# In float32 groups GpSimd multiplies the exponentials by the reciprocals of their sums, in place of VectorE

## The chip, the cores and the metric

The kernel runs on one core of one Trainium2 chip. The metric is the time of the device in microseconds: the median of several executions of the whole program. A core has a matrix engine (TensorE, in rows PE, and PEld for its weight loads), VectorE (DVE), ScalarE (ACT), GpSimd (POOL) and a queue engine that issues most transfers (SyncE, SP). Each engine takes its instructions in the order of the program, and waits for other engines by semaphores.

## The reference

Three stages follow each other, all in float32. The inputs are `q`, `k` and `v` for 4 sequences of 576 tokens with 8 heads of 64 (2304 tokens in all), and six weight matrices.

```
scores = scale * q @ k^T, masked to the last 64 positions of each row
attn   = exp(scores - max);  attn = attn / (sum(attn) + 1e-9)
x      = (attn @ v) as 2304 x 512
x      = ((x @ w1) * (x @ w2)) @ w3 @ w_out
h      = x @ w_in;   out = (h * sigmoid(h)) @ w_out2
```

The change concerns the division by the sum.

## The kernel before

**Groups.** Attention is cut into 72 groups: 18 blocks of 128 tokens by 4 pairs of heads. The first 17 groups (`plain(g)`, `PLAIN = 17`) multiply in plain float32 on TensorE; the others split each operand into a high and a low part. The change concerns the first 17 alone, "float32 groups". A group goes through these steps, each a function:

- `scores(g)`: TensorE's product (L313) into PSUM; VectorE adds the mask, scales, and takes the row's extreme, in two instructions (L327), one per head.
- `exps(g)`: ScalarE takes the exponentials in place in the tile `sm`, 128 x 2 x 192, and their sums (L338).
- `normalise(g)`: VectorE adds 1e-9 to the sums (L346), takes the reciprocals `rs` (L348), and multiplies the 384 columns of `sm` by them, each head's by its own reciprocal (L350). The second operand is `rs`, repeated 192 times along the row.
- `transposes(g)`: TensorE turns `sm` in three parts (L360), and in `split_t(g)` ScalarE copies the result out (L366).
- `values(g)`: TensorE's product with `v` (L387 to L389), copied to `xr` by ScalarE (L390).

**Their order.** The order of the program is written out by hand. `half(2g)` issues `scores(g)`, `values(g-2)`, `transposes(g-1)` with its copy, and `exps(g)`; `half(2g+1)` issues `normalise(g)` and loads for later groups. So on TensorE the transposes of a group stand behind the scores of the next group, and on ScalarE the exponentials of group g stand behind the copy of group g-1.

**The work around them.** In the first stretch, `phase_w` (some 95 us), the weights arrive as 64-bit floats and are converted to float32, 512 columns at a time: two scalings on ScalarE (L119, L120), a shift and a merging of the sign on VectorE (L130, L133), and an integer add on GpSimd (L137). Some chunks then get a high and a low part (L145 on ScalarE; L149 on VectorE or GpSimd in turn). TensorE meanwhile multiplies `w3` by `w_out` (L542). The halves of the groups 0 to 13 are spread over this stretch; the groups 14 to 16 fall into the next one, `phase_a(0)`, where TensorE's products with `w1` and `w2` begin (L576). GpSimd also takes the low parts of `x` there and here (`split`, L84).

**What fills the gaps.** A chunk's second stage is not issued at once. It is put into a list, `parts`, as two pieces: `fraction` (L130) and `sign`, and `fill()` issues the next piece. `sign` issues the merging on VectorE and, right behind it, the add on GpSimd:

```
nc.vector.scalar_tensor_tensor(out=b, in0=self.high, scalar=-0x80000000, in1=self.z, ...)
nc.gpsimd.tensor_tensor(out=x, in0=b, in1=self.r, op=ALU.add)
```

`normalise` calls `fill()` ahead of each of its three instructions.

Of the kernel before, what the change touches and what calls it, by code (L numbers as in the profile page):

```python
# [14 lines left out]
ALU = mybir.AluOpType  # L15
# [27 lines left out]
def tile_window_attention_ffn(ctx, tc, qkv, vp, mask, ident, w1, w2, w3t, w_out, w_in, w_out2, out):  # L43
# [7 lines left out]
    nc = tc.nc  # L51
# [153 lines left out]
    def fill(n=1):  # L205

        for _ in range(min(n, len(parts))):
            parts.pop(0)()
# [44 lines left out]
    def plain(g):  # L253


        return g < PLAIN
# [85 lines left out]
    def normalise(g):  # L342
        _, rs = s_st.pop(g)
        x = sm[g % 2]
        fill()
        nc.vector.tensor_reduce(out=rs, in_=sums_of[g % 2], axis=mybir.AxisListType.X, op=ALU.add)  # L346
        fill()
        nc.vector.reciprocal(out=rs, in_=rs)  # L348
        fill()
        nc.vector.tensor_tensor(out=x, in0=x, in1=rs.unsqueeze(2).to_broadcast([128, 2, 192]), op=ALU.mult)  # L350

    def transposes(g):

# [56 lines left out]
    def half(h):  # L410
# [18 lines left out]
        else:  # L429
            if g < NG:  # L430
                normalise(g)
# [639 lines left out]
```

## Time and profile before

| what | value |
|---|---|
| median of 3 runs | 844.87 us (844.01 to 845.13) |
| the profiled execution's own time | 844.38 us |
| its span in the profile | 842.6 us |
| TensorE busy | 824.5 us (98%) |
| VectorE busy | 614.4 us (73%) |
| ScalarE busy | 560.8 us (67%) |
| GpSimd busy | 530.6 us (63%) |

The span runs from the first to the last instruction of the program. A busy time is the union of an engine's instructions; TensorE's matmuls are pipelined and their ends are modelled, so that a high share says that it is rarely without work and not that it is at its peak. The shares are means over stages that differ: the changed line runs in the first 112 us alone.

### The profile page before, as it was taken

Reading aid. Unit: us, or ns where it says so; the run is one execution under the profiler, and the core shown is the slowest. Engines: PE = TensorE matmul, PEld = TensorE weight load, DVE = VectorE, ACT = ScalarE, POOL = GpSimd, SP = SyncE. Lnnn points to the kernel's source line nnn. Section 1 sums busy time; section 2 is a strip of 40 time slices with the busy share of each in tenths; the row PEclk is TensorE's granted clock in tenths of the full one; section 3 lists DMA queues with packets and bytes.
Section 4 is the critical chain, followed back from the end, with each engine's and each line's share of the span. In section 5 each row is a group of like instructions: output and inputs, shape, how many; then the busy total and the mean of one; then the engine's idle time right before and its main releaser. Section 6 shows DMA issues by size and latency. Waiting matters only on the chain.

```text
span 842.6 us, 14171 instructions
## 1 busy us (share of the span) xinstructions
PE 824.5 (98%) x4410; PEld 744.9 (88%) x4410; DVE 614.4 (73%) x1420; ACT 560.8 (67%) x1389; POOL 530.6 (63%) x588
## 2 busy tenths in 40 slices
PE   5999999999999999999999999999999999999998
PEld 2555799999999999999999998888898888888986
DVE  5879877688888888888368698998644568644544
ACT  5889778898898899898556566546543446443433
POOL 5669676677677677677465577876455457454441
PEclk9999999999999999999999999999999999999999
DMA  8999334434544554543443522301301201201001
GB/s 299 315 309 289 106 96 125 145 118 142 167 157 144 170 157 145 169 152 107 134 154 114 200 75 75 125 26 51 101 25 45 106 26 63 88 25 51 1 1 75
DMA packets 57130, 102.66 MB, mean 122 GB/s; under 512 B 5472, under 2 KB 34912, under 8 KB 57056
## 3 DMA queue, kind: packets, MB, share of 16 engines
q1 hardware_dynamic: 53600, 97.05, 35.7%
q10 hardware_dynamic: 3456, 4.72, 1.5%
q8 instruction: 35, 0.57, 0.3%
q14 instruction: 39, 0.32, 0.1%
HBM read 88.11 MB, written 13.63 MB: 121 GB/s over the span
## 4 chain that ended last, share of the span: by engine, by line
PE 68%; ACT 7%; POOL 6%; issue 4%; DVE 3%; ACTq 0%; POOLq 0%; DVEq 0%
PE o L835 22%; PE ab L576 16%; PE hy L781 11%; PE hx L781 9%; PE x L600 6%; POOL klo L296 2%; ACT sm L338 1%; PE t L360 1%; POOL xr L406 1%; POOL vhl L84 1%; ACT qkhi L292 1%; PE o L394 1%; POOL p L84 1%; PE s L317 1%; POOL q L84 1%
## 5 line engine op out<-in xcount | busy, mean ns | idle before, releaser
L835 PE MATMUL o<-hl,gp 128*128 128x512 f32 x504 | 133.3, 394 | 0.0
L576 PE MATMUL ab<-xa,hl 128*128 128x384 f32 x576 | 119.0, 341 | 0.0
L781 PE MATMUL hy<-xop,j 128*128 128x384 f32 x576 | 116.0, 335 | 0.5 <-DVE tmp L675 0.5
L576 PE MATMUL ab<-xb,hl 128*128 128x384 f32 x576 | 115.4, 334 | 0.0
L84 POOL TENSOR_TENSOR gp<-tmp,gp 128x384 fp32r<-128x384 f32 x56 | 63.5, 1134 | 79.5 <-ACT gp L81 77.9
L781 PEld LDWEIGHTS hy<-xop,j 128*128 128x128 f32 x576 | 102.7, 188 | 9.8 <-DVE tmp L675 1.6
L835 PEld LDWEIGHTS o<-hl,gp 128*128 128x128 f32 x504 | 93.1, 188 | 13.1
L576 PEld LDWEIGHTS ab<-xb,hl 128*128 128x128 f32 x576 | 101.3, 188 | 0.0
L797 ACT ACTIVATE tmp<-hx 128x384 f32<-128x384 f32 x48 | 23.6, 492 | 114.0 <-DVE hx L675 69.2
L576 PEld LDWEIGHTS ab<-xa,hl 128*128 128x128 f32 x576 | 99.1, 188 | 0.0
L675 DVE TENSOR_TENSOR tmp<-hy,tmp 128x384 f32<-128x384 f32 x96 | 53.2, 554 | 56.9 <-PE hy L781 52.0
L781 PE MATMUL hx<-xop,j 128*128 128x384 f32 x432 | 86.6, 335 | 0.0
L835 PE MATMUL o<-hl,gq 128*128 128x512 f32 x324 | 85.9, 393 | 0.0
L84 POOL TENSOR_TENSOR gq<-tmp,gq 128x384 fp32r<-128x384 f32 x36 | 40.0, 1111 | 72.6 <-ACT gq L81 72.6
L781 PEld LDWEIGHTS hx<-xop,j 128*128 128x128 f32 x432 | 76.8, 188 | 4.2
L406 POOL TENSOR_TENSOR xr<-ot 128x128 f32<-128x128 f32 x55 | 32.3, 587 | 73.9 <-DVE ot L405 65.8
L296 POOL TENSOR_TENSOR klo<-qk,qkhi 64x192 fp32r<-64x192 f32 x110 | 68.0, 618 | 7.6 <-ACT qkhi L292 2.7
L835 PEld LDWEIGHTS o<-hl,gq 128*128 128x128 f32 x324 | 60.3, 188 | 11.2
L600 PE MATMUL x<-p,wp 128*128 128x384 f32 x360 | 69.6, 339 | 0.0
L338 ACT ACTIVATE sm<-sm,nm 128x192 f32<-128x192 f32 x144 | 64.5, 450 | 3.8 <-DVE nm L327 2.4
L600 PEld LDWEIGHTS x<-p,wp 128*128 128x128 f32 x360 | 61.8, 188 | 0.0
L137 POOL TENSOR_TENSOR cv_b<-cv_b,cv_r 128x512 int32<-128x512 int32 x32 | 48.6, 1520 | 18.7 <-DVE cv_b L133 9.4
(138 smaller groups left out, 1887.4 us busy)
## 6 DMA issues: line engine op xcount, KB each, us to landing
qk<-in_qkv SPq DMA_DIRECT2D x55, 384.0 KB, 3.2
words<-in_w_out SPq DMA_DIRECT2D x24, 512.0 KB, 5.4
r<-w_in SPq DMA_DIRECT2D x22, 512.0 KB, 3.4
words<-in_w3t SPq DMA_DIRECT2D x16, 512.0 KB, 6.6
words<-in_w SPq DMA_DIRECT2D x16, 512.0 KB, 6.6
xe<-in_w_in SPq DMA_DIRECT2D x16, 512.0 KB, 4.6
v<-in_qkv SPq DMA_DIRECT2D x55, 96.0 KB, 2.7
x2d<-x2s ACTq DMA_DIRECT2D x24, 192.0 KB, 1.9
```

Of the source, the lines that this page charges most:

```text
L84: (nc.vector if eng_lo == "dve" else nc.gpsimd).tensor_tensor(out=lo, in0=src, in1=f32(hi), op=ALU.subtract)
L137: nc.gpsimd.tensor_tensor(out=x, in0=b, in1=self.r, op=ALU.add)
L292: nc.scalar.copy(out=hi, in_=t)
L296: nc.gpsimd.tensor_tensor(out=k_lo[g % 2][hs, h * 192 : h * 192 + 192], in0=t[hs, n], in1=f32(hi[hs, n]), op=ALU.subtract)
L338: nc.scalar.activation(out=x, in_=x, func=AF.Exp, scale=-1.0, bias=nm[:, h : h + 1], accum_out=sums_of[g % 2][:, h, 0:1])
L406: nc.gpsimd.tensor_tensor(out=xr[:, c, r : r + 128], in0=t[:, 0:128], in1=t[:, 128:256], op=ALU.add)
L576: nc.tensor.matmul(acc, lhsT=w[:, l, fs], rhs=x[k // 2][:, k % 2, r, :], start=(k == 0 and n == 0), stop=(k == 3 and n == 2),)
L600: nc.tensor.matmul(acc, lhsT=wp[f][:, l, o * 128 : (o + 1) * 128], rhs=p[f][:, r, :], start=(f == 0 and n == 0), stop=(f == 7 and n == 2),)
L675: eng.tensor_tensor(out=out, in0=a, in1=b, op=op)
L781: nc.tensor.matmul(bank[name], lhsT=w[:, l, at + kt], rhs=x[:, kt, r, :], start=(fresh and kt == 0 and n == 0), stop=(kt == 1 and n == 2), ...
L797: nc.scalar.activation(out=sg, in_=src, func=AF.Sigmoid)
L835: nc.tensor.matmul(oacc[t], lhsT=g[:, l, cols], rhs=weights["out", 2 * p + i][:, r, :], start=(p == 0 and i == 0 and n == 0), stop=(p == P ...
```

## The change

In the float32 groups the third instruction of `normalise` goes to GpSimd's queue. Operands, result and place in the program's order are the same; the other groups keep it on VectorE.

```diff
@@ -347,7 +347,9 @@
         fill()
         nc.vector.reciprocal(out=rs, in_=rs)
         fill()
-        nc.vector.tensor_tensor(out=x, in0=x, in1=rs.unsqueeze(2).to_broadcast([128, 2, 192]), op=ALU.mult)
+        (nc.gpsimd if plain(g) else nc.vector).tensor_tensor(
+            out=x, in0=x, in1=rs.unsqueeze(2).to_broadcast([128, 2, 192]), op=ALU.mult
+        )
```

## Rows read from the trace of the kernel before

**Rows 1.** The page: engine's busy time and share; TensorE's granted clock in 40 slices.
```profile
PE 824.5 (98%) x4410; PEld 744.9 (88%) x4410; DVE 614.4 (73%) x1420; ACT 560.8 (67%) x1389; POOL 530.6 (63%) x588
...
PEclk9999999999999999999999999999999999999999
```
**Rows 2.** Busy time by stretch: window, length, each engine's busy us (instructions), clock, DMA share.
```profile
60.00:70.00 10.00, 9.22 (x37) 5.20 (x36) 9.06 (x29) 9.73 (x27) 9.93 (x8) 1.00 0.92 294
70.00:80.00 10.00, 9.82 (x36) 5.32 (x34) 9.19 (x19) 8.75 (x21) 9.78 (x9) 1.00 0.89 287
...
120.00:140.00 20.00, 20.00 (x129) 20.00 (x128) 14.91 (x54) 16.23 (x49) 11.49 (x18) 1.00 0.35 103
```
**Rows 3.** Groups of the first 100 us: busy us, mean ns | idle before, releasers.
```profile
L137 POOL TENSOR_TENSOR cv_b<-cv_b,cv_r 128x512 int32<-128x512 int32 x14 | 20.1, 1435 | 10.0 <-DVE rs L348 3.6 <-DVE rs L346 2.7 <-ACT cv_r L120 2.3
...
L350 DVE TENSOR_TENSOR sm<-sm,rs 128x384 f32<-128x384 f32 x15 | 10.2, 677 | 0.5
...
L360 PE MATMUL t<-id_sb,sm 128*128 128x128 f32 x42 | 7.1, 278 | 3.8 <-DVE sm L350 1.5 <-ACT cv_b L119 1.3 <-ACT cv_r L120 0.8
...
L84 POOL TENSOR_TENSOR xa<-xr,xa 128x384 fp32r<-128x384 f32 x2 | 2.0, 1008 | 0.0
```
**Rows 4.** Order of time around group 1: start us, duration us, engine and line.
```profile
19.50 0.69 DVE L133 SCALAR_TENSOR_TENSOR cv_b<-words,cv_z 128x512 int32<-128x512 int32 x1
...
20.30 0.56 DVE L350 TENSOR_TENSOR sm<-sm,rs 128x384 f32<-128x384 f32 x1
20.34 1.66 POOL L137 TENSOR_TENSOR wo<-cv_b,cv_r 128x512 int32<-128x512 int32 x1 [0.35 <-DVE rs L348]
...
21.01 0.52 PE L360 MATMUL t<-id_sb,sm 128*128 128x128 f32 x3 [0.75 <-DVE sm L350]
...
23.35 0.42 ACT L366 COPY pw<-t 128x320 f32<-128x320 f32 x1
```
**Rows 5.** Order of time, VectorE: the multiplications of groups 5, 7, 8, 11, 13.
```profile
44.00 0.56 DVE L350 TENSOR_TENSOR sm<-sm,rs 128x384 f32<-128x384 f32 x1
...
55.17 0.56 DVE L350 TENSOR_TENSOR sm<-sm,rs 128x384 f32<-128x384 f32 x1
...
62.12 0.56 DVE L350 TENSOR_TENSOR sm<-sm,rs 128x384 f32<-128x384 f32 x1
...
79.03 1.35 DVE L350 TENSOR_TENSOR sm<-sm,rs 128x384 f32<-128x384 f32 x1
...
90.44 0.56 DVE L350 TENSOR_TENSOR sm<-sm,rs 128x384 f32<-128x384 f32 x1
```
**Rows 6.** Order of time, TensorE: transposes of groups 4, 5, 7, 8, 11, 13.
```profile
39.98 0.50 PE L360 MATMUL t<-id_sb,sm 128*128 128x128 f32 x3
...
45.02 0.50 PE L360 MATMUL t<-id_sb,sm 128*128 128x128 f32 x3
...
56.79 0.50 PE L360 MATMUL t<-id_sb,sm 128*128 128x128 f32 x3
...
62.82 0.52 PE L360 MATMUL t<-id_sb,sm 128*128 128x128 f32 x3 [0.78 <-ACT cv_r L120]
...
80.53 0.52 PE L360 MATMUL t<-id_sb,sm 128*128 128x128 f32 x3 [0.71 <-DVE sm L350]
...
94.35 0.50 PE L360 MATMUL t<-id_sb,sm 128*128 128x128 f32 x3
```
**Rows 7.** Order of time, GpSimd: two adds ahead of group 11's transposes.
```profile
78.70 1.26 POOL L137 TENSOR_TENSOR cv_b<-cv_b,cv_r 128x512 int32<-128x512 int32 x1
79.92 1.61 POOL L137 TENSOR_TENSOR q<-cv_b,cv_r 128x512 int32<-128x512 int32 x1
```
**Rows 8.** Order of time, ScalarE: copies of groups 4 and 7, exponentials of group 8.
```profile
40.52 0.43 ACT L366 COPY pw<-t 128x320 f32<-128x320 f32 x1
...
58.25 0.46 ACT L366 COPY pw<-t 128x320 f32<-128x320 f32 x1
60.20 0.46 ACT L338 ACTIVATE sm<-sm,nm 128x192 f32<-128x192 f32 x1 [1.49 <-DVE nm L327]
```

## The prediction

> **What bounds the kernel now.** I read the page first. TensorE is busy for 98% of the span and is granted nine tenths or more of its clock in every slice, the 2.4 GHz level [rows 1], so the time is TensorE's work plus its pauses: 842.6 - 824.5 leaves 18 us of pauses in all. An engine other than TensorE matters only where TensorE waits for it. Next I read the busy time by stretch: the changed line runs only in the first 112 us, where weight conversion, TensorE's float32 products and the 17 float32 groups run together. There TensorE still has small gaps, GpSimd varies between much room and none (9.93 and 9.78 busy of 10 between 60 and 80 us), and VectorE is above 8 of 10 [rows 2]. From 120 us on TensorE has no gap at all in the stretch shown [rows 2]. A pause added to TensorE before 112 us can therefore not be made good later: it is added to the end. The question is how long TensorE waits in front of the 17 sets of transposes.
>
> Third, the groups of instructions of the first 100 us [rows 3]. The transposes (L360) have 3.8 us of idle in front of them, mostly put down to the multiplication (L350). That is the price of the chain today. Fourth, the order of time around single groups, which carries the sum.
>
> **The pattern of one group.** In `normalise`, `fill()` stands between the reduction, the reciprocal and the multiplication. In the groups 1 to 13 one of these fills issues a `sign` part: its VectorE half (L133) runs between reduction and reciprocal, and its GpSimd half (the integer add, L137) is issued right behind it, thus ahead of the multiplication. Group 1 shows it [rows 4]: L133 19.50 to 20.19, reciprocal, L350 20.30 to 20.86, transposes at 21.01. GpSimd's add starts at 20.34, at the same moment as L350. On VectorE the multiplication doesn't see this add. On GpSimd it stands behind it.
>
> **The change, part by part.**
> Removed: 17 multiplications on VectorE. The unhindered one takes 0.56 us [rows 4]; the mean over the first 15 is 677 ns [rows 3]. Together 11.5 us of VectorE's time, none of it on TensorE directly.
> Added: 17 multiplications on GpSimd. The trace has no product on GpSimd, and none with an operand repeated along the row. The nearest row is the subtraction of the same 128x384 elements (L84), 1008 ns [rows 3]. I take 1.0 us. Below, the 0.56 us of VectorE bounds it; above I take 1.6 us, about the longest add of [rows 4], since nothing shows what the repeated operand costs. The Trainium skill speaks against the change: GPSIMD Engine Reference, 4.1 Engine selection, gives elementwise work on a tile to VectorE, with GpSimd about twice as slow for two inputs; 1.0 against 0.56 agrees, and with exactly twice the sum below would be some 1 us higher (an estimate).
> Moved: the wait. GpSimd now waits for the reciprocal; behind that wait stand only later adds, whose VectorE halves come later anyway. TensorE waits for GpSimd in place of VectorE. No DMA is moved.
> Given back: add and multiplication no longer stretch each other. In group 1 the add took 1.66 us because L350 ran [rows 4]; unhindered it is about 1.28 (the add at 78.70 took 1.26 [rows 7]). So GpSimd pays 1.0 and gets 0.38 back where they met. The Trainium skill (SBUF, State Buffer, section SBUF: two separate sides) says that VectorE with two SBUF inputs and GpSimd exclude each other for the whole instruction; the stretched add agrees. This gift is in the sum.
>
> **The payment of a group.** Count from the end of L133. Before: L350 ends 0.67 later (20.86 - 20.19), the transposes start 0.15 after that: 0.82. After: 0.15 from VectorE to GpSimd (20.19 to 20.34), the add 1.27, the multiplication 1.0, and 0.15 to TensorE: 2.57. The transposes become possible 1.75 us later. How much TensorE feels is 1.75 less the room that the group had: start of the transposes less the end of L350 less 0.15.
> The rooms, from the starts of L350 and of the transposes [rows 5, 6]: group 1 none; 5: 45.02 - 44.56 - 0.15 = 0.3; 7: 0.9; 8 none; 11 none; 13: 3.2. Worked out in the same way from the two views, groups 2, 3 and 12 have none, 4 has 1.25, 6 1.55, 9 0.85, 10 1.55; 0, 14 and 15 more than 1; 16 none, but its queue neighbour is short of the usual add, at most 0.6.
>
> **Who pays again.** If each group paid anew, the sum of 1.75 less room is 4 x 1.75 (groups 1, 2, 3, 8) + 2 x 1.75 (11, 12) + 0.5 + 1.45 + 0.2 + 0.85 + 0.9 + 0.2 + 0.6 = 15.2 us. That is the upper end. But once TensorE is late, a later group whose own chain isn't late hides the next delay. The link back is ScalarE's copy L366, which follows the transposes and stands ahead of the next group's exponentials.
> - Group 1 pays 1.75.
> - Groups 2 to 4 pay nothing: ScalarE reaches the copy at 23.35 [rows 4], 1.8 us after the transposes of group 1 were done (21.53), so the chain of group 2 keeps its time; TensorE, late by 1.75, meets a multiplication late by 1.75. Group 3 is the same; 4 has 1.25 of room and VectorE is behind there anyway.
> - From group 5 the copy follows at once (40.52 [rows 8], after transposes that end at 40.48 [rows 6]), chain and TensorE are late together: 5 pays 1.45, 6 0.2, 7 0.85.
> - Group 8: its exponentials wait at 60.20 for VectorE and not for the copy at 58.25 [rows 8], so the chain is less late than TensorE; against that GpSimd's queue is full. Walking the three queues forward, each row starting when its engine and its last input are ready, I get 1.0 of the 1.75. Groups 9 and 10 then pay 0.15 each by the same walk.
> - Group 11: two adds follow each other on GpSimd, at 78.70 and 79.92 [rows 7], the second ahead of the multiplication: 79.92 + 1.27 + 1.0 + 0.15 = 82.35 against 80.53: 1.8, and 0.4 for the queue that is full since 60 us [rows 2]. Group 12 follows from a chain less late than TensorE and pays nothing.
> - 13 to 16 pay nothing (room, or the same reason).
> Sum: 1.75 + 1.45 + 0.2 + 0.85 + 1.0 + 0.3 + 2.2 = 7.75 us. VectorE's freed time is inside it, as the slack of groups 4, 8 and 12.
> The profiled execution took 844.38 us (span 842.6 and 1.8 around it), the median is 844.87. 844.38 + 7.75 = 852.1, and 0.5 for the median: 852.6 us.
> Low bound of this case: groups 8 to 12 pay once 1.75 between them and the rest stands, 6.0 us: 850.9; with a multiplication of 0.8 us, 0.2 less at some nine paying places: 849.1. High bound: 1.3 us at the same places, 2.7 more: 855.3.
>
> **The rivals.**
> - *Every group pays anew* (15.2 us, 860.1): it needs every chain to be as late as TensorE. Against it stand the two ScalarE rows of groups 2 and 8. 0.06.
> - *The product with a repeated operand is dear on GpSimd*: at 1.6 us nine places pay 0.6 more, 7.75 + 5.4 = 13.2: 858.1. For it: no row shows this form. Against it: the subtraction over 384 and the add over 512 elements (1.0 and 1.27 us) differ as their widths do, whatever the operation. 0.10.
> - *Hidden anyway*, within 0.2% (1.7 us, about what a measurement of this kernel can tell from no change): the late transposes would have to fall into pauses that TensorE has for other reasons. Only the two waits not put down to L350, 1.3 and 0.8 [rows 3], offer that: 7.75 - 2.1 is still 5.6. 0.05; its time is 845.5.
> - *Faster*, the other side: VectorE, above 8 of 10 busy, is the real brake; its 11.5 us and GpSimd's 0.38 per meeting bring the adds earlier and the 3.8 us in front of L360 go: 841.0. It decides only if the multiplication ends less than 0.67 us after L133, which the add ahead of it (1.27) excludes in the groups 1 to 13. 0.05.
>
> **How the numbers follow.** The forecast case has 0.74. Slower: 0.74 + 0.06 + 0.10 = 0.90; same 0.05; faster 0.05. The range runs from 848.5, under the low bound, to 858.0, taking in most of the dear product; outside lie faster, same and the case in which each pays anew, 0.16, and some of the dear one.
>
> **What would show it.** The product on GpSimd at 1.0 us, starting where the add L137 ends and not at the reciprocal. The transposes waiting for GpSimd, with some 11.5 us of idle in front of them in place of 3.8. The copies and exponentials of groups 2 and 3 at their old times. GpSimd's adds at 1.28 in place of 1.66. From 120 us on everything shifted by one constant. The forecast is wrong if the product stands ahead of the add in GpSimd's queue (then it pays about 0.5 per group), or if it is not near 1.0 us.

## The result, and the profile after

| kernel | median (range), runs | ratio to before, 95% interval |
|---|---|---|
| before | 845.08 us (844.01 to 846.4), 6 | |
| changed | 853.07 us (850.92 to 854.2), 6 | 1.0096 [1.0085, 1.0107] |

The change costs 8.0 us. The profiled execution took 851.4 us, with a span of 849.6 where before had 842.6, 7.0 more. Executions of the changed kernel differ more among themselves than those of before, and in step with TensorE's mean clock: the one with a clock of 1.000 took 850.92, those with 0.995 to 0.997 took 852.85 to 854.2.

The page of the changed kernel, engines and granted clock, beside [rows 1]:

```profile
PE 826.7 (97%) x4410; PEld 745.8 (88%) x4410; DVE 603.2 (71%) x1403; ACT 561.5 (66%) x1389; POOL 538.8 (63%) x605
...
PEclk9999999999999999999999999999999999999999
```

VectorE lost 11.2 us of work, and GpSimd has only 8.2 us more, although 17 products (14.5 us) came to it: its adds no longer meet VectorE's multiplication, and the 40 adds L137 of the first 125 us take 51.5 us in place of 56.5. TensorE runs the same 4410 matmuls, but is busy 2.2 us longer. Of the 7.0 us of the span 4.8 are thus pauses, and the rest slower matmuls (shown below). The groups of the first 108 us (lines below the diff are two higher: L362 are the transposes, L368 the copy, L544 the products with `w_out`), beside [rows 3]:

```profile
L137 POOL TENSOR_TENSOR cv_b<-cv_b,cv_r 128x512 int32<-128x512 int32 x14 | 18.1, 1294 | 9.0 <-DVE rs L348 5.1 <-DVE rs L346 3.8 <-DVE cv_b L133 0.2
...
L350 POOL TENSOR_TENSOR sm<-sm,rs 128x384 f32<-128x384 f32 x15 | 12.8, 855 | 2.5 <-DVE rs L348 2.5
...
L362 PE MATMUL t<-id_sb,sm 128*128 128x128 f32 x45 | 7.9, 283 | 8.2 <-POOL sm L350 8.1
```

The pauses before the transposes went from 3.8 to 8.2 us, now put down to GpSimd's product. A product takes 0.82 us unhindered (855 ns in the mean), and the add of this row is at 1.29 in the mean where it was at 1.44. Group 1 in order of time, GpSimd and TensorE, beside [rows 4]:

```profile
21.02 1.27 POOL L137 TENSOR_TENSOR wo<-cv_b,cv_r 128x512 int32<-128x512 int32 x1 [0.47 <-DVE rs L348]
22.25 0.83 POOL L350 TENSOR_TENSOR sm<-sm,rs 128x384 f32<-128x384 f32 x1
...
23.13 0.55 PE L362 MATMUL t<-id_sb,sm 128*128 128x128 f32 x3 [2.25 <-POOL sm L350]
...
23.52 5.30 PE L544 MATMUL accw<-wo,q 128*128 128x512 f32 x8
```

The product starts as the add ends, at 22.25; the reciprocal was ready at 20.95. TensorE stands for 2.25 us, 1.50 more than before. The last row holds something that the prediction doesn't know: eight matmuls took 5.30 us, which took 3.60 before:

```profile
21.36 3.60 PE L542 MATMUL accw<-wo,q 128*128 128x512 f32 x8
```

Busy time by stretch, around it and in tens of us, the clock being the column after POOL's:

```profile
20.00:22.00 2.00, 0.88 (x7) 0.64 (x5) 1.61 (x5) 1.23 (x2) 1.52 (x2) 1.00 0.99 293
22.00:24.00 2.00, 0.87 (x5) 0.64 (x6) 1.85 (x6) 1.68 (x4) 2.00 (x3) 1.00 0.98 311
24.00:26.00 2.00, 2.00 (x4) 0.81 (x3) 0.92 (x4) 2.00 (x7) 0.31 (x2) 0.58 0.88 287
26.00:28.00 2.00, 2.00 (x4) 0.86 (x3) 1.40 (x3) 1.71 (x4) 2.00 (x2) 0.56 1.03 400
28.00:30.00 2.00, 2.00 (x11) 1.28 (x10) 1.72 (x5) 1.31 (x3) 1.74 (x3) 1.00 1.07 364
...
80.00:90.00 10.00, 6.91 (x24) 3.69 (x23) 6.60 (x16) 6.94 (x18) 8.79 (x7) 1.00 0.75 229
...
88.00:90.00 2.00, 2.00 (x7) 0.96 (x6) 0.46 (x2) 1.80 (x7) 0.79 (x1) 1.00 0.98 297
```

After the pause TensorE was granted 0.56 to 0.58 of its clock, thus mostly the 1.2 GHz level, for some 4 us, and then all of it again. The slices of the page are too coarse to show it. In this execution the fall costs little: group 2's transposes are 3.6 us late, group 3's 1.8 again, because TensorE no longer has to wait there. The transposes of group 3, before and after:

```profile
33.22 0.52 PE L360 MATMUL t<-id_sb,sm 128*128 128x128 f32 x3 [1.31 <-ACT cv_b L119]
...
34.97 0.55 PE L362 MATMUL t<-id_sb,sm 128*128 128x128 f32 x3
```

Group 11, the largest single loss, on GpSimd and TensorE:

```profile
83.83 1.26 POOL L137 TENSOR_TENSOR cv_b<-cv_b,cv_r 128x512 int32<-128x512 int32 x1
85.05 1.27 POOL L137 TENSOR_TENSOR q<-cv_b,cv_r 128x512 int32<-128x512 int32 x1
86.28 1.27 POOL L350 TENSOR_TENSOR sm<-sm,rs 128x384 f32<-128x384 f32 x1
87.52 1.26 POOL L137 TENSOR_TENSOR cv_b<-cv_b,cv_r 128x512 int32<-128x512 int32 x1
...
87.61 0.55 PE L362 MATMUL t<-id_sb,sm 128*128 128x128 f32 x3 [3.09 <-POOL sm L350]
```

Its reciprocal, before and after:

```profile
78.84 0.16 DVE L348 RECIPROCAL rs<-rs 128x2 f32<-128x2 f32 x1
...
83.97 0.16 DVE L348 RECIPROCAL rs<-rs 128x2 f32<-128x2 f32 x1
```

The reciprocal is ready at 84.13, but two adds keep GpSimd until 86.3, and the product then takes 1.27 us.

The start of each group's transposes, after less before [rows 6], gives TensorE's lateness: group 1 2.1 us, 2 3.6, 3 and 4 1.8, 5 2.9, 6 3.2, 7 3.7, 8 to 10 4.4 to 4.7, 11 7.1, 12 to 16 6.7 to 6.8. Of group 1's 2.1, some 0.6 were there ahead of its add: VectorE's reduction starts 0.7 us later than before, and so do, by 0.6, the scores on TensorE that stand in front of these transposes and wait for their load. The scores, before and after:

```profile
18.76 0.88 PE L313 MATMUL s<-kp,qp 128*128 128x384 f32 x2 [0.20 <-DMA kp<-in_qkv]
...
19.38 0.88 PE L313 MATMUL s<-kp,qp 128*128 128x384 f32 x2 [0.41 <-DMA kp<-in_qkv]
```

In a run below (group 1 alone on VectorE), whose work is the same up to this time, these scores start at 18.41. Single traces thus differ by up to 1 us from execution to execution; the growth from one group to the next says more than the lateness itself.

### The profile page after: what moved, and what is told of

The parts are those of the page before. It is cut to its first block, busy times and chain, and to the rows that moved or that the text cites. A ratio compares the mean times of both kernels' runs of the same rounds, so it can differ in the third digit from the quotient of the medians.

```text
span 849.6 us, 14208 instructions
## 1 busy us (share of the span) xinstructions
PE 826.7 (97%) x4410; PEld 745.8 (88%) x4410; DVE 603.2 (71%) x1403; ACT 561.5 (66%) x1389; POOL 538.8 (63%) x605
## 4 chain that ended last, share of the span: by engine, by line
PE 68%; POOL 8%; ACT 7%; issue 5%; DVE 3%; ACTq 0%; POOLq 0%; DVEq 0%
PE o L837 22%; PE ab L578 14%; PE hy L783 11%; PE hx L783 8%; PE x L602 6%; POOL klo L296 2%; PE t L362 1%; ACT sm L338 1%; POOL xr L408 1%; POOL vhl L84 1%; POOL p L84 1%; PE accw L544 1%; ACT qkhi L292 1%; PE o L396 1%; POOL q L84 1%
## 5 line engine op out<-in xcount | busy, mean ns | idle before, releaser
L677 DVE TENSOR_TENSOR tmp<-hy,tmp 128x384 f32<-128x384 f32 x96 | 53.2, 554 | 56.5 <-PE hy L783 51.9
L837 PEld LDWEIGHTS o<-hl,gq 128*128 128x128 f32 x324 | 60.3, 188 | 11.2
L137 POOL TENSOR_TENSOR cv_b<-cv_b,cv_r 128x512 int32<-128x512 int32 x32 | 46.7, 1460 | 17.8 <-DVE cv_b L133 8.4
```

The costliest lines, as they stand in the source:

```text
L677: eng.tensor_tensor(out=out, in0=a, in1=b, op=op)
L837: nc.tensor.matmul(oacc[t], lhsT=g[:, l, cols], rhs=weights["out", 2 * p + i][:, r, :], start=(p == 0 and i == 0 and n == 0), stop=(p == P ...
```

## The experiments

Three theories were put against each other. A: the product waits behind an add in GpSimd's queue. B: GpSimd's 14 us of new work delay the weights. C: the product is longer on GpSimd and lies on the chain. From the second series on, theory D joins A and B, each for its own stretch.

**The product ahead of the add.** GpSimd's half of `sign` is held back inside `normalise` and issued after the product; VectorE's order is that of the changed kernel.

```diff
-                nc.gpsimd.tensor_tensor(out=x, in0=b, in1=self.r, op=ALU.add)
+                add = lambda: nc.gpsimd.tensor_tensor(out=x, in0=b, in1=self.r, op=ALU.add)
+                held.append(add) if hold[0] else add()
...
+        hold[0] = plain(g)
         fill()
...
         (nc.gpsimd if plain(g) else nc.vector).tensor_tensor(
             out=x, in0=x, in1=rs.unsqueeze(2).to_broadcast([128, 2, 192]), op=ALU.mult
         )
+        hold[0] = False
+        while held:
+            held.pop(0)()
```

> The multiplication stays on GpSimd in the float32 groups, but an add L137 that a fill issues inside normalise is put behind it in GpSimd's queue; VectorE's order is the same as in the changed kernel. Before takes 845.1 us, the changed kernel 853.1. Theory A (the wait behind the add costs the time): from the end of the reciprocal the product is now 0.15 + 0.82 + 0.15 against 0.03 + 0.56 + 0.15 before, 0.4 per paying group instead of 1.6; with four or five paying groups 846 to 847.5 us, and the pause of 2.25 us before the second transposes shrinks under 1.3. Rival B (GpSimd's load: 14 us more work delays the weights' adds): the load is the same, so at least 851. Rival C (the product is simply longer on GpSimd and lies on the chain: 17 x 0.26 = 4.5 us): 849 to 850.

849.16 us against 844.98, ratio 1.0047 [1.0035, 1.006]: half of the loss is gone, the other half not. The trace says where each half lies. The transposes of the groups 1 to 10 stand at most 0.1 us later than before, from group 3 on 0.4 to 0.6 earlier (group 0 already stands 0.7 earlier in this execution, so this is no gain). So in these groups the queue position was the whole loss, and theory C falls: 0.82 in place of 0.56 us costs nothing there. Then comes group 11. GpSimd (product L353) and TensorE (transposes L368, products L550) in order of time:

```profile
77.14 1.30 POOL L150 TENSOR_TENSOR hl<-cv_b,hl 128x512 fp32r<-128x512 f32 x1
78.37 1.29 POOL L137 TENSOR_TENSOR cv_b<-cv_b,cv_r 128x512 int32<-128x512 int32 x1
81.78 0.83 POOL L353 TENSOR_TENSOR sm<-sm,rs 128x384 f32<-128x384 f32 x1 [2.12 <-DVE rs L351]
...
82.66 0.90 PE L368 MATMUL t<-id_sb,sm 128*128 128x128 f32 x3 [3.27 <-POOL sm L353]
83.36 6.17 PE L550 MATMUL accw<-wo,w3x 128*128 128x512 f32 x8
```

The busy time of the same kernel by stretch, from 60 us on and after the pause:

```profile
60.00:70.00 10.00, 9.15 (x37) 5.28 (x36) 7.60 (x22) 9.33 (x25) 10.00 (x10) 1.00 0.90 266
70.00:80.00 10.00, 9.39 (x35) 5.13 (x33) 8.16 (x13) 8.84 (x20) 9.66 (x9) 1.00 0.93 320
...
84.00:86.00 2.00, 2.00 (x4) 0.76 (x3) 1.97 (x6) 2.00 (x8) 1.57 (x2) 0.50 0.80 297
86.00:88.00 2.00, 2.00 (x4) 0.93 (x3) 1.20 (x2) 1.66 (x4) 2.00 (x3) 0.50 0.14 57
```

GpSimd has no gap from 57.8 to 79.7 us. In group 11 the reciprocal itself is 2.6 us late. What makes it late is a chunk's low part, which stands ahead of it on VectorE (L149 before, L150 here):

```profile
76.49 1.11 DVE L149 TENSOR_TENSOR hl<-cv_b,hl 128x512 fp32r<-128x512 f32 x1 [0.36 <-ACT hl L145]
...
76.65 3.56 DVE L150 TENSOR_TENSOR hl<-cv_b,hl 128x512 fp32r<-128x512 f32 x1 [1.25 <-ACT hl L146]
```

It starts 0.16 us later than before and takes 3.56 us in place of 1.11: three instructions of GpSimd follow each other until 79.66, and the subtraction ends 0.55 us after the last of them. Before, it ended 0.55 us after the first. TensorE stands for 3.27 us, its clock falls to half, and eight matmuls take 6.17 us. The lateness goes from -0.4 at group 10 to 2.1 at group 11 (the pause) and 4.8 at group 12 (the clock).

**All fills behind, on VectorE.** VectorE keeps the product, and in the float32 groups `normalise` calls its three `fill()` after it.

```diff
-        fill()
+        late = 3 * plain(g)
+        fill(1 if not late else 0)
         nc.vector.tensor_reduce(out=rs, in_=sums_of[g % 2], axis=mybir.AxisListType.X, op=ALU.add)
-        fill()
+        fill(1 if not late else 0)
         nc.vector.reciprocal(out=rs, in_=rs)
-        fill()
+        fill(1 if not late else 0)
         nc.vector.tensor_tensor(out=x, in0=x, in1=rs.unsqueeze(2).to_broadcast([128, 2, 192]), op=ALU.mult)
+        fill(late)
```

> VectorE keeps the multiplication, and in the float32 groups the three fills of normalise come after the multiplication instead of ahead of its three instructions, so that nothing stands between reduction, reciprocal and multiplication on VectorE. Theory A (what counts is what stands between the sums and the transposes): the chain is shorter by L133 (0.6) and, where it stood there, L130 (0.7); TensorE's 3.8 us of waits before L360 shrink, 842 to 844 us. Rival B (the adds count): they come 0.8 us later in each group and TensorE waits for them: 845 to 848. If the order inside normalise is without weight: 845.

852.25 us, 1.0085 [1.0071, 1.0099]: against theory A as I applied it, nearly as slow as the change without a single product on GpSimd. Two rows of its waits (what waits, for what: us, times, longest), and the same two of the kernel before:

```profile
ACT sm L338 <- DVE nm L327: 11.3, 8, 1.9
...
DVE rs L347 <- ACT sm L338: 7.0, 6, 2.8
```

```profile
DVE rs L346 <- ACT sm L338: 4.4, 6, 2.0
...
ACT sm L338 <- DVE nm L327: 2.4, 3, 1.5
```

VectorE stands idle until the sums come (7.0 us in place of 4.4), and the work that used to cover this wait now stands in front of the next mask step, for which ScalarE waits (11.3 in place of 2.4). A shorter chain within a group is no gain if the cover is lost.

**A product that nobody reads.** The kernel before, plus a product of the same size on GpSimd on a spare tile of zeros in the groups 0 to 14.

```diff
+    spare = att.tile([128, 768], F32, name="spare", tag="qk", bufs=2)[:, 0:384].rearrange("p (h n) -> p h n", h=2)
+    nc.vector.memset(spare, 0.0)
...
+        if g < 15:
+            nc.gpsimd.tensor_tensor(
+                out=spare, in0=spare, in1=rs.unsqueeze(2).to_broadcast([128, 2, 192]), op=ALU.mult
+            )
         nc.vector.tensor_tensor(out=x, in0=x, in1=rs.unsqueeze(2).to_broadcast([128, 2, 192]), op=ALU.mult)
```

> The kernel before, with the multiplication on VectorE, and one more product on GpSimd of the same size in the groups 0 to 14, on a spare tile of zeros with the same reciprocals, whose result nobody reads. It has the changed kernel's load on GpSimd in 15 of 17 groups and none of its waits. Theory A (the wait): 845 to 846.5 us. Rival B (the load): 850 or more. Rival C (length of the product on the chain): 845.

847.62 us, 1.0031 [1.0019, 1.0044]: between what A and B expected, and both in part. From group 3 to group 10 its transposes are 0.4 us late; then GpSimd is full and TensorE pauses once, in group 11, before its clock falls. The busy time of this kernel by stretch:

```profile
60.00:70.00 10.00, 9.17 (x37) 5.26 (x36) 9.27 (x28) 9.03 (x24) 10.00 (x10) 1.00 0.97 317
70.00:80.00 10.00, 10.00 (x37) 5.40 (x35) 8.21 (x17) 8.82 (x23) 10.00 (x9) 1.00 0.91 299
80.00:90.00 10.00, 7.44 (x26) 4.03 (x25) 9.19 (x24) 7.18 (x17) 9.64 (x8) 0.83 0.52 165
```

VectorE's low part ahead of group 11, and TensorE behind it, in order of time (transposes L366, products L548):

```profile
78.77 1.10 DVE L149 TENSOR_TENSOR hl<-cv_b,hl 128x512 fp32r<-128x512 f32 x1 [1.14 <-ACT hl L145]
...
82.80 0.52 PE L366 MATMUL t<-id_sb,sm 128*128 128x128 f32 x3 [2.56 <-DVE sm L356]
83.15 5.29 PE L548 MATMUL accw<-wo,w3x 128*128 128x512 f32 x8
```

Here the low part is not stretched, but starts 2.3 us later than before (76.49): it waits for ScalarE's high part, and this for GpSimd's add. The executions with a clock of 1.000 took 846.83 to 847.14 us, those with 0.998 took 848.11 to 848.73: the load costs about 2.1 us, the fall of the clock behind it another 1.5.

**Only groups with room.**

```diff
-        (nc.gpsimd if plain(g) else nc.vector).tensor_tensor(
+        (nc.gpsimd if g in (0, 6, 10, 13, 14, 15) else nc.vector).tensor_tensor(
```

> Only the groups 0, 6, 10, 13, 14 and 15 multiply on GpSimd, the six with the most room before their transposes; the other eleven stay on VectorE. Theory A with the rooms of the prediction: at most 0.4 us more, 845.1 to 845.6. Proportional to the number of groups (rivals B and C): 6/17 of 8.0 us, 2.8 more, 847.9.

845.19 us, 1.0003 [0.9993, 1.0013]: no measurable difference, as A expected; a loss in proportion to the groups is excluded.

**Both causes taken away.** The product ahead of the add, and the groups 8 to 11 on VectorE: the two conditions `plain(g)` become `plain(g) and not 7 < g < 12`.

> As the kernel with the multiplication put ahead of the add, but the groups 8 to 11 keep it on VectorE (and their adds where they were), so that GpSimd has no products between 60 and 82 us, where it has no gap. Theory D (two causes: the queue position in the groups 1 to 8, and GpSimd's load in the stretch 60 to 82 us, which delays group 11 and is followed by a fall of TensorE's clock): with both taken away 844 to 845.5 us, before being 845.0. If the 4.2 us that were left came from the product's length on GpSimd in any group: 847.5 to 848.5.

844.76 us, 1.0008 [0.9999, 1.0017]: the loss is gone. Thirteen of the 17 products are on GpSimd and cost nothing that can be measured. TensorE's pauses before the transposes are back at 4.0 us:

```profile
L368 PE MATMUL t<-id_sb,sm 128*128 128x128 f32 x42 | 7.6, 292 | 4.0 <-POOL sm L353 2.7 <-DVE sm L353 1.3
```

**Load taken off GpSimd in another way.** The product ahead of the add in all 17 groups, and the low parts L149 of the first stretch all on VectorE (twice `(nc.vector,)` for `(nc.vector, nc.gpsimd)` in the calls of `steps_to` in `phase_w`); and as a control the kernel before with this second edit alone.

> As the kernel with the multiplication put ahead of the add in all 17 groups, and the low parts L149 of the first stretch all on VectorE in place of every second one on GpSimd: 1.3 us each off GpSimd, six of them before 82 us, against 0.8 us each for its products. Theory D (load of GpSimd at 60 to 82 us): group 11 finds the queue as in the kernel before, 843.5 to 845.5. If VectorE becomes the brake: 846 or more.

> The control: the kernel before, with the low parts L149 of the first stretch all on VectorE. VectorE is 9 of 10 busy there and gets 6 x 0.7 us more, and GpSimd 6 x 1.3 less. If VectorE is the brake in this stretch 846 to 849 us, if GpSimd's full queue at 60 to 82 us is what group 11 waits for already before, 844 to 845.

845.37 us, 1.0014 [1.0005, 1.0023], with all 17 products on GpSimd; the control 850.66, 1.0075 [1.0062, 1.0087]. VectorE can take the low parts only once it has given up the products: in the control it is busy for 9.6 to 9.8 of every 10 us between 60 and 90 us. This exchange too removes the loss that group 11 had with the turned order (group 11 adds 0.1 us to the lateness here), and confirms that it came from GpSimd's load; 1.0 us over before stays, and nothing is won.

**Queue position without load.** The changed kernel with `g < 8` for `plain(g)`: the products of the groups 0 to 7 behind the add, none later.

> The changed kernel with only the groups 0 to 7 on GpSimd, the multiplication behind the add as the change has it. Theory D: the queue position alone, without products in the full stretch: the shift that the changed kernel's trace shows at the transposes of group 7, 3.7 us, so 847.5 to 849; walking the rows with 0.82 us gives 2.2, 847.2. If the load of the full stretch made it all, 845 to 846.

848.2 us, 1.0043 [1.003, 1.0055], 3.8 us above the runs of before beside it (844.37). The lateness is 4.9 us at group 7 and stays at 4.0 from group 8 on; group 11 adds nothing. Here, too, TensorE's clock falls behind a pause, of 2.29 us in group 1:

```profile
24.00:26.00 2.00, 2.00 (x3) 0.78 (x3) 1.44 (x6) 2.00 (x7) 1.27 (x1) 0.50 1.01 369
```

All five executions have a clock of 0.996 to 0.998. The 3.8 us are therefore the queue position together with the fall of the clock that follows it; the walk along the rows with 0.82 us gave 2.2 for the position alone.

**Group 1 alone on VectorE** (`plain(g) and g != 1`), the other sixteen as changed.

> The changed kernel with group 1 alone kept on VectorE. If each group pays for itself (1.75 us at group 1, 2.1 in the changed kernel's trace), 851 us, 2 less than the 853.1 of the change. If a late TensorE hides the next delay, group 3 pays in place of group 1 and little is won: the walk gives 0.0, 853 us. If the pause of 2.25 us before the transposes of group 1 and the fall of the clock behind it are what varies from run to run, the pause becomes shorter and the clock stays at full speed between 20 and 30 us.

852.44 us, 1.0096 [1.008, 1.0112]: no gain that the runs can tell from the change. In its trace the pause of 2.25 us and the fall of the clock between 20 and 30 us are gone, group 2 pays 1.2 and the lateness at group 10 is 3.1 in place of 4.7. Then group 11 pays as ever, and in this execution the clock falls after that pause. The one execution with a clock of 1.000 took 850.82 here, and 850.92 with the change. So group 1 does not simply pay for itself: then the loss would have been some 2 us smaller, and it is 7.8. Whether its part is 0, as the walk gave, or up to 1.5, as this one trace up to group 10 has it, stays open; single traces differ by up to 1 us there, as seen above.

**One fill ahead, two behind**, on VectorE, and on GpSimd for all float32 groups but 8 to 11:

```diff
         fill()
         nc.vector.tensor_reduce(out=rs, in_=sums_of[g % 2], axis=mybir.AxisListType.X, op=ALU.add)
-        fill()
+        fill(0 if plain(g) else 1)
         nc.vector.reciprocal(out=rs, in_=rs)
-        fill()
+        fill(0 if plain(g) else 1)
         nc.vector.tensor_tensor(out=x, in0=x, in1=rs.unsqueeze(2).to_broadcast([128, 2, 192]), op=ALU.mult)
+        fill(2 if plain(g) else 0)
```

> VectorE keeps the multiplication; in the float32 groups the first fill of normalise stays ahead of the reduction and the other two come after the multiplication. The work that covers the wait for the sums stays, and the chain loses L133 (0.6 us), which also brings the add behind the multiplication. If the kernel with all three fills behind lost its 7.3 us because VectorE then stood idle while it waited for the sums: 843 to 845 us (before: 844.7). If it lost them because adds come later: 846 to 849.

> The same order of fills, with the multiplication on GpSimd in all float32 groups but 8 to 11. Product ahead of the add, chain shorter by L133, full stretch without products. Theory D: 843 to 845 us, as the one on VectorE or 0.5 less, for VectorE's freed time. If the length of GpSimd's product matters once the chain is short: 0.5 to 1.5 more than the one on VectorE.

845.25 us, 1.0007 [0.9998, 1.0016], and 845.09, 1.0006 [0.9997, 1.0015]. The first fill is what the version with all three behind had lost: 7 us lie between the two. A chain that is 0.6 us shorter gains nothing, on neither engine. No version tried beats the kernel before.

## Why the prediction was right, and where it wasn't

- *TensorE alone sets the time, and a pause before 112 us is not made good.* Right for the sum: the lateness of 6.8 us at group 12 is that of the groups behind it, and the span is 7.0 longer. But TensorE's own waits before 112 us can swallow some: 1.8 us of group 2's lateness are gone at group 3.
- *The product stands behind the add.* Right, and shown: with the order of the two turned, the groups 1 to 10 lose nothing; with the position kept and no load later (groups 0 to 7), 3.8 us are lost, the fall of the clock included.
- *The product takes 1.0 us.* It takes 0.82. The nearest row, the subtraction with a rounded result, was not near enough, and a product not near 1.0 us is one of the two signs by which the forecast calls itself wrong. With 0.18 us less at the prediction's nine paying places, 6.1 us are left of its 7.75.
- *Who pays again.* Right in kind. Predicted and found: group 1 1.75 and 2.1 (its pause grew by 1.5); 2 to 4 none, and 0.3 less; 5 1.45 and 1.1; 6 0.2 and 0.3; 7 0.85 and 0.5; 8 1.0 and 0.7; 9 and 10 0.3 and 0.3; 11 and 12 together 2.2 and 2.2; 13 to 16 nothing and nothing. That each group pays anew is excluded by the trace, and the measured 8.0 us stand against its 15.2.
- *Group 11.* In the changed kernel's own trace both size and reason hold. I put 1.8 of its 2.2 down to the two adds ahead of the product and 0.4 to the queue. From the end of the reciprocal to the transposes it is 3.5 us in place of 1.5, 1.95 more: two adds, then the product, which takes 1.27 us in place of 0.82 beside a subtraction on VectorE (L149, 86.10 to 86.88). The reciprocal itself is 0.5 later than the lateness of group 10 gives. What the prediction didn't see is a second loss of the same size that waits behind the first. With the product ahead of the add, group 11 still lost 2.6 us; with a product that nobody waits for, 1.9; without products in that stretch, nothing. This second loss is GpSimd's load, 60 to 82 us [rows 2], and it reaches TensorE through a low part on VectorE, which was stretched in the one case and started late in the other. The changed kernel's own queue has gaps there, because its products wait for reciprocals:

```profile
70.05 1.28 POOL L137 TENSOR_TENSOR cv_b<-cv_b,cv_r 128x512 int32<-128x512 int32 x1 [0.46 <-DVE rs L348]
...
75.45 1.28 POOL L137 TENSOR_TENSOR cv_b<-cv_b,cv_r 128x512 int32<-128x512 int32 x1 [0.88 <-DVE rs L348]
```

- *What the sum didn't hold.* TensorE's clock falls to 1.2 GHz after some of the longer pauses. In the changed kernel the executions at a clock of 1.000 and at 0.995 to 0.997 lie 2 to 3 us apart. The Trainium skill (TensorE: Matmul & The Clock Gate, section Why this matters for your kernels) advises against idle gaps between bursts of matmuls for this reason; the rows here agree in kind, at pauses of 2.25 to 3.27 us, though the pause of 3.09 us in the changed kernel had no fall behind it. The idle time in front of the transposes, forecast at some 11.5 us, came out at 8.2, in part because 2.2 us of the loss are slower matmuls and not pauses.

That the 852.6 us came out so near the 853.07 is partly luck, two errors against each other: a product 0.18 us too dear at nine places, 1.6 us, and a fall of the clock that was left out, some 2 us in the median. The one execution of the changed kernel at a clock of 1.000 lost 5.8 us (850.92 - 845.08), near the 6.1 that the sum gives with the right product. In the profiled execution the fall behind group 1 was swallowed; where it stayed in the slower ones was not traced.

The parts by experiment: products behind an add in the groups 0 to 7 cost 3.8 us; products ahead of the add, in the stretch where GpSimd is full, cost 4.2 (849.16 - 844.98); without both, nothing is lost. Both figures hold a fall of the clock. That 3.8 and 4.2 make the 8.0 of the change is no proof that they are its two parts: turning the order also frees the groups 8 to 10, which lost 1.0 in the changed kernel, and brings the low part of 3.56 us, which takes 1.10 there. How the loss of the changed kernel behind group 7 divides between queue position, load and clock stays open. The unread product alone has 2.6 of the 4.2: by the traces group 11 loses 1.9 with it and 2.6 with the turned order, and the clock 1.4 and 2.6.

*Faster* fell on its condition, as stated: the product can't end within 0.67 us of L133 behind an add of 1.27. *Dear product* fell with the 0.82 us.

## What to carry to other kernels

An instruction that moves to another engine takes the place in that engine's queue at which the program issues it: look at what is issued just ahead, since 0.26 us more of work cost nothing here and 1.27 us of a foreign add, in the groups 0 to 7, cost 3.8 us in all. A queue that is full in one stretch must be counted by stretch, not by its mean share of 63%. Its damage showed at another engine: VectorE's low part started 2.3 us late in one kernel and took 3.56 us in place of 1.11 in another. Before shortening a chain by moving fillers, see which of them cover a wait.

## What was not expected of the hardware

- GpSimd multiplies 128x384 floats by an operand repeated along the row in 0.82 us, quicker than it subtracts two full operands into the rounded type (1.00 us).
- A subtraction on VectorE ended only 0.55 us after the last of three GpSimd instructions that followed each other without a gap, and took 3.56 us; before it ended 0.55 us after the first of them, and took 1.11. What decides between the two isn't settled by these rows.
- TensorE's clock fell to half after a pause of 2.25 us (0.56 to 0.58 for 4 us, the changed kernel at 24 us), of 3.27 (0.50 for some 6 us), of 2.56 and of 3.06 (group 1 alone on VectorE, at 86 us), but not after one of 3.09 us in the changed kernel at 87 us. Eight matmuls then took 5.3 to 6.2 us in place of 3.6. What decides isn't settled by these rows.
